# Attention and mixer on one core: fillers moved to a bank of their own, transposes and weight loads moved by a place

## The chip, the cores and the metric

The kernel runs on one core of a Trainium2 chip. The metric is the device time of one launch in microseconds (us). The engines are named as the profile names them: PE (TensorE, matrix multiplications; PEld is its loading of weights), DVE (VectorE), ACT (ScalarE), POOL (GpSimd) and SP (which here only starts transfers). POOL also starts transfers: those of the weights.

## What is computed

The reference, cut to what matters:

```python
q_n, k_n = rmsnorm(q, g_q), rmsnorm(k, g_k)          # (8, 12, 448, 64)
attn = softmax(q_n @ k_n^T / 8)                       # per batch and head
x = (attn @ v) as (8, 448, 768)
h = x^T @ U @ V                                       # rank 32, over the 448 tokens
u = x + h^T
out = u + relu(u @ w_ch1) @ w_ch2                     # 768 -> 3072 -> 768
```

Matrix multiplications run in bf16 and accumulate in fp32; inputs and output are fp32.

## The kernel before

**Stages.** Eight batches pass through attention, mixing (the rank-32 product) and the two-layer perceptron. The perceptron of batch b is PE's main work; the attention of batch b+1 is cut into small pieces that are woven into it. `weave` does that: it emits pieces of the perceptron (six matmuls each) until their volume reaches the share that is due by the weights of the attention's pieces, then one piece of the attention. The fraction of the perceptron over which a batch's attention is spread is `FA` (0.74 for even batches, 0.77 for odd), and `FM` (0.09) is that of the mixing that follows it. Each engine executes its own instructions in the order in which they were emitted; the program is scheduled by hand.

**The head.** Batch 0 has no perceptron to be woven into. Its order is a list written out by hand, `plan` in `head` (L659 to L867): normalise queries and keys (squares, reduce, rsqrt, scale), transpose them on PE (`turn`, L259, with the copies `keep`, L266), scores (L291), exponentials (`expo`, L301, on ACT), the product with the values (`weigh`, L307), its division by the sums (`normalise`, L327), and the mixing (`gather`, `spread`). `heat(n)` (L902) puts n fillers into PE's order: matmuls of zeros, 512 columns wide, whose result nobody reads. Each call takes a buffer of the pool `ps_mm`, which has three and which also serves transposes, products and the perceptron.

**A visit.** `attention(b)` (L575) emits six visits for a batch, one for each pair of heads p. A visit holds the scores for the four blocks of keys (two and two), their exponentials, the values of the pair before, and the preparation of the next pairs. `transposes(p)` turns the scaled queries and keys: on PE up to p = 13, by a transposing DMA from SP from p = 14 (`NPE`) on. Squares of heads 16 to 23 run on POOL (L233); later ones on ACT (L231).

**Two engines and one order.** `yield_port` (L568) is a copy of one element on POOL that reads what a `scale` on DVE (L253) writes, so that what stands behind it on POOL does not begin before that scale is done.

**Weights.** The first weights come in four loads, `load_w1(0)` to `load_w1(3)` (hidden columns up to 512, 1024, 2048 and 3072), the second in six, `load_w2`, all started by POOL. `load_w1(2)` holds what hidden blocks 8 to 15 of the perceptron need. The second weights 1 to 5 are started from the visits 6, 7 and 8 of batch 1's attention (`late`, L914).

**Mixing.** `mix_u` adds the low-rank term (DVE, L378); `mix_uT` turns each of the four blocks of rows by a transposing DMA from SP (L385). The perceptron of that batch begins with the result. Output blocks are stored by SP as well (`store`, L430).

**PSUM.** The pool `ps_o` has one bank; it holds `o`, the product with the values, 260 of the bank's 512 columns, before it is normalised.

Of the kernel before, what the change touches and what calls it, by code (L numbers as in the profile page):

```python
# [9 lines left out]
FP32 = mybir.dt.float32  # L10
# [7 lines left out]
def kernel(  # L18
# [13 lines left out]
    nc = tc.nc  # L32
    B, H, S, D = q.shape
# [5 lines left out]
    P = 128  # L39
# [26 lines left out]
    ps_mm = ctx.enter_context(tc.tile_pool(name="ps_mm", bufs=3, space=bass.MemoryType.PSUM))  # L66
    ps_s = ctx.enter_context(tc.tile_pool(name="ps_s", bufs=2, space=bass.MemoryType.PSUM))
    ps_o = ctx.enter_context(tc.tile_pool(name="ps_o", bufs=1, space=bass.MemoryType.PSUM))

    ident = consts.tile([P, P], BF16, name="ident")  # L70
    w1b = consts.tile([P, KD, dh], BF16, name="w1b")
# [17 lines left out]
    FA, FM, NPE, FA0, FL = (0.74, 0.77), 0.09, 14, 0.66, 0.2  # L89
# [20 lines left out]
    def E_of(p):  # L110
        return Es[p % 3 if p < 6 else p % 2]

    def va_of(t):
        return vas[t if t < 3 else (t + 1) % 2]
# [3 lines left out]
    cold = ring[:, 0, :]  # L118
# [73 lines left out]
    NT, NP = B * 3, B * 6  # L192
# [114 lines left out]
    def weigh(p, hh):  # L307

        b = p // 6
        par, g = b % 2, b // 2 % 2  # L310
        E, va = E_of(p), va_of(p // 2)
        hl = 2 * (p % 2) + hh
        if hh and p < 6:
            o = ps_mm.tile([P, 4, D + 1], FP32, tag="mm")
        elif hh and p % 6 == 5:
            o = ps_s.tile([P, 4, D + 1], FP32, tag="s", name="o")
        else:
            o = ps_o.tile([P, 4, D + 1], FP32, tag="o")
        for i, off in enumerate(OFFS[par]):
            n = (i + 1) % 4 if par == 0 and g else i  # L320
            for kc in range(NJ):
                c = PAD + kc * S + off
                nc.tensor.matmul(o[:, n, :], E[:, hh, c:c + P], va[:, hl, kc, :],  # L323
                                 start=(kc == 0), stop=(kc == NJ - 1))
        outs[p, hh] = o
# [18 lines left out]
    def values(p, hh):  # L344

        weigh(p, hh)
        normalise(p, hh)
# [227 lines left out]
    def attention(b, extra={}, later=None):  # L575

        items = []

        def add(weight, fn, *args):
            put = items if later is None or args[0] < ahead.get(fn, NP) else later  # L580
            put.append((weight, lambda: fn(*args)))

        def late_add(fn, *args):
            later.append((0, lambda: fn(*args)))

        def idle():
            pass

        def sums(p, n):
            f = {12: 0, 13: 1, 14: 3, 15: 2}.get(p)  # L590
            if f is not None:
                add(0, weight_sums, f, 3 * n)

        for p in range(b * 6, b * 6 + 6):
            t, odd = divmod(p, 2)
            more, more2 = t + 1 < NT, t + 2 < NT
            add(2 if p == 6 else 1, scores, p, (0, 1))
            add(0, expo, p, 0)
            add(.5, expo, p, 1)
            if p + 1 < NP and (p + 1 >= NPE or not odd):  # L600
                add(.5, transposes, p + 1)
            if 7 <= p <= 10:
                add(0, mix_u, 0, p - 7, (0,))
            sums(p, 0)
            lead = 1 if b == 1 else 2
            if not odd and p > 9 and t + lead < NT:
                add(0, load, t + lead, 1, (0,))
            if not odd and more:
                add(0, squares, t + 1, ALL, (1,))
            if odd and more2:  # L610
                add(0, squares, t + 2, ALL, (0,))
            if p % 6:
                add(2, values, p - 1, 0)
            elif b > 1:
                add(1, idle)
            sums(p, 1)
            if not odd and more:
                add(0, reduce, t + 1, ALL, (1,))
            if odd and more:
                add(0, scale, t + 1, 1)  # L620
                add(0, yield_port, t + 1, 1)
                add(0, cast_v, t + 1)
            if odd and 6 <= t + lead < NT:
                add(0, load, t + lead, 1, (1,))
            add(1, scores, p, (2, 3))
            add(0, expo, p, 2)
            add(.5, expo, p, 3)
            if p + 1 < NPE and odd:
                add(.5, transposes, p + 1)
            if 7 <= p <= 10:  # L630
                add(0, mix_u, 0, p - 7, (1,))
            if p + 1 < NP:
                add(0, gains, p + 1)
            if not odd and more:
                add(0, rsqrt, t + 1)
            sums(p, 2)
            if p % 6:
                add(1.5, values, p - 1, 1)
            elif b > 1:
                add(1, idle)  # L640
            sums(p, 3)
            if not odd and more:
                add(0, scale, t + 1, 0)
                add(0, yield_port, t + 1, 0)
            if odd and more2:
                add(0, reduce, t + 2, ALL, (0,))
            if odd and 6 <= t + lead < NT:
                add(0, load_v, t + lead)
            if p in extra:
                add(0, *extra[p])  # L650
            if p == 11:
                add(0, load, 7, 1, (0,))
                late_add(load, 7, 1, (1,))
                late_add(load_v, 7)
        add(2, values, b * 6 + 5, 0)
        add(2, values, b * 6 + 5, 1)
        return items

    def head():  # L659
# [13 lines left out]
        cast_u = lambda: nc.gpsimd.tensor_copy(Uc, Uf)  # L673
        pool = nc.gpsimd
        plan = [
            (heat, 16),
            (grow2,),
            (squares, 0, A, (0,), pool),
            (squares, 0, A, (1,)),
            (squares, 0, Bh, (0,), pool),  # L680
            (reduce, 0, A, (0,)),
            (reduce, 0, A, (1,)),
# [2 lines left out]
            (squares, 0, Bh, (1,)),  # L685
            (scale, 0, 0, (1,)),
            (reduce, 0, Bh, (1,)),
            (scale, 0, 0, (0,)),
            (rsqrt, 0, Bh),
            (scale, 0, 1, (1,)),  # L690
# [3 lines left out]
            (keep, 0, 0, 1),  # L694
            (yield_port, 0, 1),
            (squares, 1, ALL, (1,)),
            (keep, 0, 1),
            (scale, 0, 1, (0,)),
            (heat, 4),
            (scores, 0, (0,)),  # L700
            (turn, 1),
            (squares, 2, ALL, (0,)),
# [2 lines left out]
            (scores, 0, (1,)),  # L705
            (reduce, 1, ALL, (1,)),
            (load_w1, 0),
            (expo, 0, 1),
            (rsqrt, 1),
            (heat, 2),  # L710
            (scores, 0, (2,)),
            (scores, 0, (3,)),
            (keep, 1, 1),
# [2 lines left out]
            (squares, 2, ALL, (1,)),  # L716
            (scale, 1, 0, (0,)),
            (expo, 0, 2),
            (scale, 1, 1, (1,)),
            (heat, 5),  # L720
            (scores, 1, (0,)),
            (turn, 2),
            (scale, 1, 1, (0,)),
            (expo, 0, 3),
            (cast_u,),
            (expo, 1, 0),
            (scores, 1, (1,)),
            (scores, 1, (2,)),
            (load, 4),
            (heat, 2),  # L730
            (turn, 3),
# [5 lines left out]
            (expo, 1, 3),  # L737
            (scores, 2, (0,)),
            (yield_port, 1, 0),
            (scores, 2, (1,)),  # L740
            (cast_v, 0),
            (expo, 2, 0),
            (expo, 2, 1),
            (reduce, 2, ALL, (0,)),
            (reduce, 2, ALL, (1,)),
            (setup_u, 0),
            (scores, 2, (2,)),
            (scores, 2, (3,)),
# [141 lines left out]
    def weave(fill, total, items):  # L890
        weights = sum(w for w, _ in items)
        done = due = 0.0
        for w, piece in items:
            due += w * total / max(weights, 1)
            while done < due:
                n = next(fill, None)
                if n is None:
                    break
                done += n
            piece()  # L900

    def heat(n):  # L902
        if n:
            warm = ps_mm.tile([P, 512], FP32, tag="mm")
            for _ in range(n):
                nc.tensor.matmul(warm, cold[:, 0:P], cold[:, 0:512], start=True, stop=True)

    def volume(b):
        n = (384, 512)[b % 2]
        return (24 if b else 20) * n + (28 if b % 2 else 22 if b else 24) * HALF  # L910

    with tc.manual_schedule():
        head()
        late = {6: (load_w2s, 1, 3), 7: (load_w2s, 3, 5), 8: (load_w2s, 5, 6)}  # L914
        for b in range(B):
            fill, total = mlp(b), volume(b)
            if b + 1 < B:
                later = []
                rest = [(4, lambda: (load_w2(0, 0), transposes(6), reduce(4, ALL, (0,))))] + attention(1, late, later)
                weave(fill, total * (FA[b % 2] if b else FA0), attention(b + 1) if b else rest)  # L920
                weave(fill, total * FM, mixing(b + 1))
                if b == 0:
                    weave(fill, total * FL, [(5 if w == .5 else 1, piece) for w, piece in later])
            for _ in fill:
                pass
# [30 lines left out]
```

## Time and profile before

| | |
|---|---|
| time before, median of 5 runs | 579.99 us (577.8 to 581.91) |
| the profiled execution: its time | 581.91 us |
| its span (first to last record) | 580.1 us |
| mean granted PE clock | 0.987 |
| busy: PE, DVE, ACT, POOL | 561.8, 389.5, 281.6, 80.1 us |
| matmuls, instructions in all | 4585, 11284 |
| moved by DMA | 67.22 MB, mean 116 GB/s |

The profiled execution is the slowest of the five, 1.92 us over their median. A row of a timeline gives the start, the duration, the engine, the line of the kernel, the operation with its output and inputs, the count, and, in brackets, how long the engine stood idle before and what ended that. In a table by windows, each engine has its busy time in the window with the number of its instructions, and PEclk is the clock granted to PE as a share of full speed. "DMA" there is the mean busy share of 16 DMA engines; it can pass 1 where packets overlap.

### The profile page before, as it was taken

The numbers are of one execution on the slowest core, as the hardware profiler recorded it, in microseconds if no ns is written. First come the engines' busy times: TensorE is split into PE (matmuls) and PEld (weight loads), VectorE is DVE, ScalarE is ACT, GpSimd is POOL, SyncE is SP. The second block draws the span as 40 slices with busy tenths as digits, with TensorE's granted clock in tenths as the row PEclk, the third lists the DMA queues.
The fourth block names the chain that finished last, engine by engine and source line by source line (L and its number), as shares of the span: only waits on it lengthen the run. The fifth ranks groups of instructions, "written<-read, shape, count | busy, mean of one in ns | idle before, by whom it ended". The sixth has DMA issues, their size and how long they took to land.

```text
span 580.1 us, 11284 instructions
## 1 busy us (share of the span) xinstructions
PE 561.8 (97%) x4585; PEld 307.6 (53%) x4607; DVE 389.5 (67%) x755; ACT 281.6 (49%) x419; POOL 80.1 (14%) x124
## 2 busy tenths in 40 slices
PE   6798999999999999999999999999999999999997
PEld 2364555544565555544456555544456555654464
DVE  5885874889975687747777498747767487453342
ACT  4686554276631786166651677246661475302200
POOL 4672610100020000000020000000001000000010
PEclk9689999999999999999999999999999999999999
DMA  9999994445544455544525444455234541050021
GB/s 207 223 243 230 211 165 124 98 124 113 127 113 99 112 131 114 128 118 112 128 63 116 116 129 112 121 142 128 69 81 129 130 97 33 28 110 1 1 55 55
DMA packets 103648, 67.22 MB, mean 116 GB/s; under 512 B 54716, under 2 KB 102060, under 8 KB 103596
## 3 DMA queue, kind: packets, MB, share of 16 engines
q1 hardware_dynamic: 93988, 56.77, 41.4%
q0 software_dynamic: 9376, 9.44, 9.8%
q8 instruction: 36, 0.59, 0.4%
q10 hardware_dynamic: 232, 0.30, 0.1%
q14 instruction: 16, 0.13, 0.1%
HBM read 52.19 MB, written 11.01 MB: 109 GB/s over the span
## 4 chain that ended last, share of the span: by engine, by line
PE 83%; DVE 5%; DMA 5%; ACT 2%; issue 1%; SPq 0%; POOL 0%; DVEq 0%; ACTq 0%
PE ph L538 35%; PE pb L463 10%; PE o L323 8%; PE pe L463 7%; PE pa L463 7%; PE sc L297 7%; PE po L463 7%; DMA w1b<-in_moe_w_ch_dram 3%; DVE qkn L253 2%; PE pu L376 2%; ACT E L302 1%; DVE ring L378 1%; DMA qk<-in_q_dram 1%; DMA u<-ring 1%; DVE rstd L239 1%
## 5 line engine op out<-in xcount | busy, mean ns | idle before, releaser
L538 PE MATMUL ph<-u,w1b 128*128 128x384 bf16 (+1 forms) x1107 | 230.8, 353 | 4.5 <-DVE qkT L275 1.2
L302 ACT ACTIVATE E<-sc 112x896 bf16<-112x896 f32 x184 | 160.0, 915 | 63.6 <-PE sc L297 63.5
L538 PEld LDWEIGHTS <-w1b 128*128 128x128 bf16 x1128 | 102.9, 98 | 111.6 <-issue 23.2
L463 PEld LDWEIGHTS <-hT 128*128 128x128 bf16 x1080 | 101.1, 98 | 71.1 <-issue 9.0
L541 ACT ACTIVATE hT<-ph 128x384 bf16<-128x384 f32 (+1 forms) x95 | 51.6, 543 | 131.3 <-PE ph L538 129.2
L543 DVE TENSOR_SCALAR hT<-ph 128x512 bf16<-128x512 f32 (+1 forms) x93 | 57.8, 622 | 56.6 <-PE ph L538 56.4
L323 PEld LDWEIGHTS <-E 112*128 112x128 bf16 x1472 | 59.8, 99 | 14.7 <-DVE ring L340 1.1
L253 DVE TENSOR_TENSOR qkn<-qk,rstd 112x512 bf16<-112x512 f32 x84 | 58.4, 733 | 7.2 <-ACT rstd L245 3.8
L323 PE MATMUL o<-va,E 112*128 112x65 bf16 x1440 | 62.1, 196 | 0.0
L297 PE MATMUL sc<-qkT 64*128 64x448 bf16 x384 | 56.7, 365 | 3.6 <-ACT E L302 1.7
L570 POOL COPY scratch<-qkn 1x1 bf16<-1x1 bf16 x44 | 11.6, 264 | 314.1 <-DVE qkn L253 314.1
L463 PE MATMUL po<-w2b,hT 128*128 128x384 bf16 x288 | 52.8, 326 | 0.1
L239 DVE TENSOR_REDUCE rstd<-sq 112x16 f32<-112x1024 f32 x40 | 48.4, 1211 | 5.1 <-ACT sq L231 5.1
L463 PE MATMUL pa<-w2b,hT 128*128 128x384 bf16 x264 | 49.5, 326 | 0.0
L463 PE MATMUL pb<-Tw,hT 128*128 128x384 bf16 x264 | 48.0, 326 | 0.0
L231 ACT ACTIVATE sq<-qk 112x1024 f32<-112x1024 f32 x36 | 38.2, 1062 | 8.1 <-DVE rstd L239 5.2
L378 DVE TENSOR_TENSOR ring<-pu,ring 128x768 bf16<-128x768 f32 (+3 forms) x36 | 31.0, 864 | 14.4 <-PE pu L376 13.8
L340 DVE TENSOR_TENSOR ring<-o,rec 128x256 bf16<-128x256 f32 (+1 forms) x96 | 37.5, 391 | 2.4
L333 DVE RECIPROCAL rec<-o 128x4 f32<-128x4 f32 x96 | 17.1, 178 | 32.5 <-PE o L323 32.0
L498 POOL TENSOR_TENSOR o<-o,ring 128x384 f32<-128x384 f32 x11 | 12.6, 1145 | 161.4 <-DVE o L497 161.4
L297 PEld LDWEIGHTS <-qkT 64*128 64x128 bf16 x384 | 12.6, 94 | 35.6 <-issue 32.0
L478 ACT ACTIVATE pb<-pa 128x384 f32<-128x384 f32 x11 | 5.2, 475 | 49.6 <-PE pa L463 49.6
(104 smaller groups left out, 428.3 us busy)
## 6 DMA issues: line engine op xcount, KB each, us to landing
qk<-in_k_dram SPq DMA_DIRECT2D x21, 448.0 KB, 5.2
vt<-in_v_dram SPq DMA_DIRECT2D x20, 448.0 KB, 4.5
qk<-in_q_dram SPq DMA_DIRECT2D x19, 448.0 KB, 3.8
w2b<-in_moe_w_ch_dram POOLq DMA_DIRECT2D x6, 768.0 KB, 15.7
w1b<-in_moe_w_ch_dram POOLq DMA_DIRECT2D x2, 1536.0 KB, 18.7
out_dram<-o SPq DMA_DIRECT2D x15, 168.0 KB, 2.3
out_dram<-o SPq DMA_DIRECT2D x16, 144.0 KB, 2.2
out_dram<-o SPq DMA_DIRECT2D x15, 120.0 KB, 2.1
```

The costliest lines, as they stand in the source:

```text
L231: nc.scalar.activation(sqs[t, s][:, hs], qks[t, s][:, hs], AF.Square)
L239: nc.vector.tensor_reduce(rstds[t][:, s, hs].rearrange("p h j -> p (h j)"), sqs[t, s][:, hs].rearrange("p h (j d) -> p (h j) d", d=D), AX, ...
L253: nc.vector.tensor_tensor(qkn[:, s].rearrange("p j h d -> p h j d"), qks[t, s][:, hp].rearrange("p h (j d) -> p h j d", d=D), rstd[:, s, h ...
L297: nc.tensor.matmul(sc[:, hh, 0:S], kT[pp, kc * SP:kc * SP + P], qT[pp, :], start=True, stop=True)
L302: nc.scalar.activation(E_of(p)[:, :, PAD + kc * S:PAD + (kc + 1) * S], scs.pop((p, kc))[0:SP, :, 0:S], AF.Exp, scale=float(D) ** 0.5)
L323: nc.tensor.matmul(o[:, n, :], E[:, hh, c:c + P], va[:, hl, kc, :], start=(kc == 0), stop=(kc == NJ - 1))
L340: nc.vector.tensor_tensor(ring[:, r0:r0 + t1 - t0, d0:d0 + D], o[:, t0:t1, 0:D], rec[:, t0:t1].rearrange("p c -> p c ()").to_broadcast([P, ...
L378: nc.vector.tensor_add(xv, pu[rows, 0:n, 0:HALF], xv)
L463: nc.tensor.matmul(ps, lhs[:, c, :], rhs[:, c, :], start=first and c == 0, stop=last and c == NC - 1, skip_group_check=again)
L538: nc.tensor.matmul(ph, w1b[:, dc, hc * P:(hc + 1) * P], u[:, dc, :], start=(dc == 0), stop=(dc == KD - 1))
L541: nc.scalar.activation(hT[:, hc, 0:n], ph, AF.Relu)
L543: nc.vector.tensor_relu(hT[:, hc, 0:n], ph)
```

## The change

- **Fillers.** `o` of the pool `ps_o` becomes the first 260 columns of a fixed bank, and the fillers write columns 272 to 511 of that bank, 240 wide, instead of taking a buffer of `ps_mm`. Their counts and places in `plan` are new: 29 fillers of 512 columns become 117 of 240. In PE's order before the first product with the values there are now 49 before the first transpose, 11 before the first scores, then 5, 18, 13, 8, 9 and 4 between the scores and transposes that follow. No filler stands behind a product with the values.
- **Transposes by DMA.** From p = 14 on, `transposes(p + 1)` stands ahead of the first two scores of visit p, and its weight (0.5) with it; it stood behind them. So the scores stand half a weight later within the visit, which moves most of them one piece of six matmuls back.
- **Second weights.** Loads 1 to 5 stand behind the squares of a visit and ahead of the values, in visits 7, 8 and 9, where they ended visits 6, 7 and 8. On POOL this swaps each pair of loads with the square that followed it: load, load, square becomes square, load, load, at two places. The fifth load keeps its place among POOL's instructions.
- **The last attention.** The attention of batch 7 is spread over 0.72 of the perceptron of batch 6, not 0.74.

On PE the rest of the head keeps its order. In the last mixing, all four blocks of `mix_u` stand one piece of six matmuls earlier, and on SP the fourth transpose of `u` stands ahead of two output stores that it followed. DVE then adds the last block before the difference L490 and the sum L492, where it came after them.

```diff
+    bank = ps_o.tile([P, 512], FP32, name="bank")
+    even = bank[:, 0:4 * (D + 1)].rearrange("p (i d) -> p i d", i=4)
+    warm = bank[:, 272:512]
...
-            o = ps_o.tile([P, 4, D + 1], FP32, tag="o")
+            o = even
...
         for p in range(b * 6, b * 6 + 6):
...
+            if NPE <= p + 1 < NP:
+                add(.5, transposes, p + 1)
             add(2 if p == 6 else 1, scores, p, (0, 1))
             add(0, expo, p, 0)
             add(.5, expo, p, 1)
-            if p + 1 < NP and (p + 1 >= NPE or not odd):
+            if p + 1 < NPE and not odd:
                 add(.5, transposes, p + 1)
...
             if odd and more2:
                 add(0, squares, t + 2, ALL, (0,))
+            if p in extra:
+                add(0, *extra[p])
             if p % 6:
                 add(2, values, p - 1, 0)
...
-            if p in extra:
-                add(0, *extra[p])
...
         plan = [
-            (heat, 16),
+            (heat, 34),
...
+            (heat, 6),
...
+            (heat, 9),
...
             (squares, 1, ALL, (1,)),
+            (heat, 11),
...
-            (heat, 4),
...
             (load_w1, 0),
+            (heat, 5),
...
-            (heat, 2),
...
             (expo, 0, 2),
+            (heat, 18),
             (scale, 1, 1, (1,)),
-            (heat, 5),
             (scores, 1, (0,)),
             (turn, 2),
             (scale, 1, 1, (0,)),
             (expo, 0, 3),
+            (heat, 9),
+            (heat, 3),
             (cast_u,),
+            (heat, 1),
             (expo, 1, 0),
             (scores, 1, (1,)),
             (scores, 1, (2,)),
+            (heat, 1),
+            (heat, 5),
             (load, 4),
             (heat, 2),
             (turn, 3),
...
             (scores, 2, (0,)),
             (yield_port, 1, 0),
+            (heat, 9),
             (scores, 2, (1,)),
...
+            (heat, 4),
             (setup_u, 0),
...
     def heat(n):
         if n:
-            warm = ps_mm.tile([P, 512], FP32, tag="mm")
             for _ in range(n):
-                nc.tensor.matmul(warm, cold[:, 0:P], cold[:, 0:512], start=True, stop=True)
+                nc.tensor.matmul(warm, cold[:, 0:P], cold[:, 0:240], start=True, stop=True)
...
-        late = {6: (load_w2s, 1, 3), 7: (load_w2s, 3, 5), 8: (load_w2s, 5, 6)}
+        late = {7: (load_w2s, 1, 3), 8: (load_w2s, 3, 5), 9: (load_w2s, 5, 6)}
...
-                weave(fill, total * (FA[b % 2] if b else FA0), attention(b + 1) if b else rest)
+                weave(fill, total * (0.72 if b == B - 2 else FA[b % 2] if b else FA0), attention(b + 1) if b else rest)
```

## The prediction

> **What bounds the kernel now.** I read the windows of ten us first, then what PE waited for, then the chain of work. From 80 us on PE is busy 99% of the time at full clock, up to the last batch. So nothing before 500 us is won unless PE stops waiting, and its waits after 40 us are few. The view of waits, PE alone, from 40 us to the end (engine, line, waited for: us in total, times, longest):
>
> ```profile
> PE ph L538 <- DVE qkT L275: 1.2, 2, 1.0
> PE ph L538 <- DMA w1b<-in_moe_w_ch_dram: 0.9, 1, 0.9
> PE ph L538 <- DMA u<-ring: 0.9, 1, 0.9
> PE sc L297 <- ACT E L302: 0.7, 1, 0.7
> PE ph L538 <- DVE hT L543: 0.5, 1, 0.5
> ```
>
> That is 4.2 us in all. The head, which most of the edits touch, shows its trouble in windows of its own (start:end, length, then busy PE, PEld, DVE, ACT, POOL, PEclk, DMA share, GB/s):
>
> ```profile
> 15.37:18.78 3.41, 1.64 (x8) 0.59 (x7) 3.41 (x4) 2.91 (x5) 3.39 (x3) 1.00 1.13 180
> 18.78:32.43 13.65, 11.94 (x112) 6.97 (x113) 11.06 (x21) 8.20 (x12) 6.91 (x10) 0.50 1.13 240
> 32.43:52.50 20.07, 20.07 (x277) 13.21 (x274) 14.52 (x35) 14.74 (x27) 10.25 (x9) 1.00 1.14 239
> ```
>
> PE is idle from 17.11 to 19.77; at 18.78 its clock halves, and stays halved to 32.43: 13.65 us at half speed. It looks like the prize. But the chain shows what stands behind it:
>
> ```profile
> 36.02 17.39 DMA w1b<-in_moe_w_ch_dram
> 53.40 0.05 issue
> 53.45 1.16 PE ph L538 x6
> ```
>
> Hidden block 8 needs the third load of the first weights, which lands at 53.40, and PE, which got there at 52.55, waits for it.
>
> **Fillers: the landing does not move.** POOL's four loads follow each other on one queue: issued at 16.21, 29.76, 36.02 and 43.39 and landing 13.8, 13.6, 17.4 and 19.9 us later, at 30.0, 43.4, 53.4 and 63.3. Each starts when the one before is done, so the third would have to be issued after 43.4 to come later, and an earlier issue brings nothing. The first is issued behind a square that waited for its data (POOL idle 3.94 for the DMA of keys), the second behind casts that waited for theirs; no step waits for PE. DMA's share is above 1 from 10 to 80 us. So what the head gains up to 53.4 becomes a longer wait there: worth between nothing and the 0.90 us of the wait itself, should the load come sooner in other executions. The ends lie close; I take the middle, **0.45**.
>
> What the head gains is needed for a rival. A filler of 240 columns isn't in the trace: between 0.033 us (the product with 65 columns, 16 in 0.52) and 0.163 (384 columns, 12 in 1.95); by columns, nearer the second, 0.102, and double at half clock. The first 49: cold as now until about 8.5, then full, ending near 10.9 (between 6.3 and 13.8) where 16 ended at 9.4. The transpose then ends 1.4 us later, but its copy on ACT stands at 11.41 behind a square that ends at 11.51 because its data came at 10.45; without that cover it would cost 1.4. The next 11 put the first scores 0.4 late, behind an exponential that waits for ACT until 13.5. The 18 fill 15.5 to 17.3 and shorten the idle time of 2.65 us to 2.0. Thirteen then delay the scores (1,1) by 1.33 us less what the clock gives the transpose. If the clock holds, ACT's nine exponentials of 0.86 and two steps of rsqrt bound the stage, and DVE is held to 29.5 by POOL's casts as now: some 1 to 1.4 us gained at 33. If it falls all the same, fillers at 0.2 us make it 1 us later, of which the wait of 0.9 covers nearly all. The fillers end before the first product in the shared bank, so they add no wait; those they took from `ps_mm` go.
>
> **Loads behind the squares.** The timelines of POOL and DVE, from two calls:
>
> ```profile
> 59.69 1.83 POOL L189 DMA_DIRECT2D w2b<-in_moe_w_ch_dram  x2
> 61.53 1.91 POOL L233 TENSOR_TENSOR sq<-qk 112x1024 f32<-112x1024 f32 x1
> ```
>
> ```profile
> 61.51 3.09 DVE L253 TENSOR_TENSOR qkn<-qk,rstd 112x512 bf16<-112x512 f32 x2
> ```
>
> Two scales take 3.09 here and 1.29 at 58.10: they stand still while POOL squares. DVE then runs without a gap, and PE waits for its copies (L275), 0.96 at 64.36 and 0.25 at 68.6. With the square first it runs from 59.65 to 61.55, before the scales, and the two issues of 1.83 beside them; that issuing alone doesn't hold them shows at 44.28, where four scales beside an issue take 2.49, 0.62 each. The copies come 1.7 us sooner, and both waits go: **1.21** (between 0 and 1.21). Next late would be DVE's relu at 79.05 (0.45); I leave it. The loads start 2 us later, the second pair 2 to 3 more because the square ahead of it waits for a reduce: behind them wait a port copy and a cast. The queue is then still busy with the load that lands at 67.7, and the products that need the last three begin near 104, where DMA's share falls after 80: no cost. If the queue did run dry, the first products at 83.4 have some 6 us left.
>
> **Spread of 0.72.** The last mixing is one piece (0.98) earlier, DVE adds the fourth block ahead of L490 and L492 (0.96 and 0.55), and SP turns it ahead of two stores (0.99). Now it is this (SP's timeline):
>
> ```profile
> 508.16 4.18 SPq L385 DMA_TRANSPOSE u<-ring  x3
> 512.44 0.99 SPq L430 DMA_DIRECT2D out_dram<-o  x2
> 513.52 1.21 SPq L385 DMA_TRANSPOSE u<-ring  x1
> ```
>
> It lands at 517.70 and PE waits from 516.88. At least 2 us sooner, it ends the wait: **0.86**; the stores move 1.2 us back, and nobody waits for them.
>
> **Transposes ahead of the scores.** Each issue (1.22) passes two output stores at most on SP and then waits for its scale, as it does now; behind it stand loads for a later visit. DVE's two waits for such transposes, 3.7 us, are off the path. What counts is where the scores come to stand. Batches 2 and 4 have one piece between two pairs of scores, PE's timeline:
>
> ```profile
> 193.12 1.15 PE L538 MATMUL ph<-u,w1b 128*128 128x384 bf16 x6
> 194.38 0.80 PE L297 MATMUL sc<-qkT 64*128 64x448 bf16 x4
> ```
>
> The scores begin 0.19 late and take 0.25 longer than the usual 0.55, since ACT has not read the buffers: 0.44, and the same at 327.4. In the new order two pieces stand there, as in batch 6 at 461.69, where nothing is lost. But ACT has a square and a relu in between, so a rest may stay: between 0 and 0.88, I take **0.70**. Elsewhere the pieces stay two or more.
>
> **Sum.** 0.45 + 1.21 + 0.86 + 0.70 = 3.22 us. The profiled execution, 581.91, would be 578.7; it lies 1.92 above the median, and taken from the median, 579.99, the sum gives **576.8**.
>
> [...] The clock stayed at half for 13.65 us though PE's rows were busy 11.94 of them, and it fell after 1.67 us of idle time. [...]
>
> **Rivals.** (1) *The clock falls in the longer wait*, slower. If the head gains 1 to 1.4, PE stands idle 1.9 to 2.3 us ahead of 53.4, more than the 1.67 after which it fell; a wait shorter than that would not decide. A fall costs half of its length: 2.7 (the first fillers, dense, were cold for 5.4) to 6.8 (half of 13.65): 579.5 to **583.6**. Against it: 11.95 to 15.37 has 1.1 us of idle time and kept its clock, and dense hidden blocks stand on both sides. Chance 0.15, with 0.06 above 582.9.
> (2) *The landing isn't the bound* in most executions; the five spread over 4.1 us. Then the head's 1.4 counts, not 0.45: 579.99 - 2.77 - 1.4 = **575.8**, down to 574.5. Chance 0.17.
> (3) *The change doesn't do what it says*: the square still meets the scales, or the new weave makes waits as large as those it removes. Then 0.86 and 0.45 are left: **578.7**. The square ends only 0.04 ahead of the scales. Chance 0.22.
> The forecast (576.2 to 577.6) has 0.46.
>
> **Numbers.** A difference of 0.5%, 2.9 us, is about what a measurement of this kernel can tell from no change; that line, 577.1, cuts through the forecast. Faster: 0.33 of the forecast and rival 2, 0.50. Slower: 0.06. The rest, 0.44, within. The range goes from 574.8 to 579.6: it leaves out rival 1 but for its low end, and the lowest of rival 2.
>
> **What would show it.** Right: PEclk 1.00 from 18 to 32 us and a longer wait for `w1b`, ending near 53.4; the scales near 61.5 at 1.3; no wait on the copies of `qkT` near 64; no wait on `u` near 515; batches 2 and 4 without late scores. Wrong: the third load landing earlier or later by over 1 us, a half clock after 50, or new waits of PE between 120 and 500 us.

## The result, and the profile after

The changed kernel takes **577.2 us** (median of 37 runs, 574.88 to 579.89); the kernel before, run beside it on the same chip, 579.84 (577.4 to 582.82). The ratio is 0.9953, with a 95% interval of 0.9943 to 0.9963: 2.6 us, or 0.47%, faster. A second measurement in another set of runs (e10 below) gave 577.01 and 0.995 [0.9931, 0.997]. The profiled execution took 576.35 us, its span is 574.6 us, its mean granted clock 1.000.

What PE waited for from 40 us to the end, as in the first list of the prediction:

```profile
PE ph L541 <- DMA u<-ring: 1.1, 1, 1.1
PE sc L300 <- ACT E L305: 0.7, 1, 0.7
PE ph L541 <- DVE hT L546: 0.4, 1, 0.4
```

The copies of `qkT` (1.2) and the first weights (0.9) are gone from it. The wait for `u` is still there, and longer; it is another one, though: it stood ahead of batch 7 and now stands ahead of batch 5, whose order in the mixing is not changed. The windows of the head (columns as in the prediction) have no half clock any more:

```profile
10.00:20.00 10.00, 7.96 (x81) 5.87 (x79) 8.60 (x12) 6.92 (x10) 6.24 (x6) 1.00 1.13 240
20.00:30.00 10.00, 9.99 (x138) 6.91 (x136) 7.81 (x18) 8.22 (x12) 4.37 (x7) 1.00 1.15 251
```

The squares and loads on POOL, and the scales on DVE, from two timelines:

```profile
56.12 1.89 POOL L236 TENSOR_TENSOR sq<-qk 112x1024 f32<-112x1024 f32 x1
57.95 1.83 POOL L192 DMA_DIRECT2D w2b<-in_moe_w_ch_dram  x2
```

```profile
58.03 1.28 DVE L256 TENSOR_TENSOR qkn<-qk,rstd 112x512 bf16<-112x512 f32 x2
```

The square ends at 58.01, the scales begin at 58.03 and take 1.28 instead of 3.09, beside the two issues. This is what the prediction described, to the order of 0.02 us. PE's timeline where batch 2 lost 0.44 us with one piece between two pairs of scores:

```profile
185.05 0.55 PE L300 MATMUL sc<-qkT 64*128 64x448 bf16 x4
185.54 2.12 PE L541 MATMUL ph<-u,w1b 128*128 128x384 bf16 x12
187.59 0.55 PE L300 MATMUL sc<-qkT 64*128 64x448 bf16 x4
```

Two pieces (2.12) stand there now, and the scores take 0.55.

How much earlier the same point of PE's work is reached than in the profile before: hidden block 0 of batch 0 by 2.5 us, block 8 by 3.5, the first product with the second weights by 5.0, the start of batch 1 by 5.0, of batch 3 by 5.6, of batch 5 by 4.9 (the new wait), of batch 7 by 5.6, the end by 5.5. That is twice what the medians show, because the two profiled executions are a late and an early one: the third load of the first weights landed at 53.4 in the one and at 49.8 (33.49 + 16.3) in the other. Whether the fillers brought any of that is open: three profiles below with the old fillers have it at 50.4 to 52.6, four with the new ones at 49.1 to 50.2 (this one among them) and a fifth at 53.1.

### The profile page after: what moved, and what is told of

Read it like the earlier page. It is cut to its first block, busy times and chain, and to the rows that moved or that the text cites. A ratio compares the mean times of both kernels' runs of the same rounds, so it can differ in the third digit from the quotient of the medians.

```text
span 574.6 us, 11445 instructions
## 1 busy us (share of the span) xinstructions
PE 561.7 (98%) x4674; PEld 314.0 (55%) x4695; DVE 385.7 (67%) x755; ACT 282.1 (49%) x419; POOL 78.9 (14%) x124
## 4 chain that ended last, share of the span: by engine, by line
PE 92%; DVE 3%; DMA 1%; ACT 1%; issue 0%; DVEq 0%; ACTq 0%
PE ph L541 38%; PE pb L466 10%; PE po L466 8%; PE sc L300 8%; PE bank L326 7%; PE pe L466 7%; PE pa L466 7%; PE pu L379 2%; PE o L326 1%; DVE qkn L256 1%; DMA u<-ring 1%; PE first L893 1%; PE pt L267 1%; PE bank L919 1%; DVE ring L381 1%; PE pm L365 1%
## 5 line engine op out<-in xcount | busy, mean ns | idle before, releaser
L256 DVE TENSOR_TENSOR qkn<-qk,rstd 112x512 bf16<-112x512 f32 x84 | 54.3, 685 | 3.9 <-ACT rstd L248 2.3
L300 PE MATMUL sc<-qkT 64*128 64x448 bf16 x384 | 54.7, 354 | 1.3 <-ACT E L305 0.7
L326 PE MATMUL bank<-va,E 112*128 112x65 bf16 x1280 | 54.1, 194 | 0.0
L343 DVE TENSOR_TENSOR ring<-bank,rec 128x192 bf16<-128x192 f32 (+1 forms) x83 | 32.3, 389 | 1.9
L336 DVE RECIPROCAL rec<-bank 128x4 f32<-128x4 f32 x83 | 14.8, 179 | 27.5 <-PE bank L326 27.2
```

Source lines behind the costliest of these rows:

```text
L256: nc.vector.tensor_tensor(qkn[:, s].rearrange("p j h d -> p h j d"), qks[t, s][:, hp].rearrange("p h (j d) -> p h j d", d=D), rstd[:, s, h ...
L300: nc.tensor.matmul(sc[:, hh, 0:S], kT[pp, kc * SP:kc * SP + P], qT[pp, :], start=True, stop=True)
L343: nc.vector.tensor_tensor(ring[:, r0:r0 + t1 - t0, d0:d0 + D], o[:, t0:t1, 0:D], rec[:, t0:t1].rearrange("p c -> p c ()").to_broadcast([P, ...
```

## The experiments

The theory after the result (Q): in the head the landing of the third load, not PE, sets when hidden block 8 can begin; so the fillers are worth nothing, and the gain is that of the moved loads and transposes. The main rival (H): the head's own work counts in most executions, and the clock that the fillers hold is worth 1 us or more. Each set of runs has its own runs of the kernel before, on the same chip: 580.6 us in the first (e1 to e4), 579.97 in the second (e5, e7 to e9), 579.79 in the third (e10 to e13). There is no e6. Ratios are to those, with 95% intervals; they are not quotients of the two medians, and gains of e1 to e4 in us are taken from the ratios.

### e1 to e4: one part of the change alone

Each is the kernel before with one part of the diff above. e1 has the bank and the new fillers:

```diff
-            (heat, 16),
+            (heat, 34),
...
+                nc.tensor.matmul(warm, cold[:, 0:P], cold[:, 0:240], start=True, stop=True)
```

> The kernel before with the fillers' part alone (the shared bank, the new counts and places). Theory Q, as in the prediction: the third load of the first weights lands by its queue, whatever the head does, so the gain is 0 to 1 us, ratio 0.998 to 1.000, and PE waits for that load longer than 0.9 us. Rival H: the landing is not what holds the head; the time gained ahead of it stays, 2 to 3.5 us, ratio 0.994 to 0.9965, and PE reaches hidden block 8 near 50 us without a wait. Both: the clock is full from 18 to 32 us in most executions.

Measured: 580.2 us (577.86 to 582.09), ratio 1.0002 [0.998, 1.0023]. Its runs show clocks of 0.994 to 1.000, those of the kernel before 0.987 to 0.997, so with the new fillers the clock holds longer, and no gain shows; the interval leaves room for 1.2 us, less than H asks for. In its profile, that of its fastest run, the load lands at 49.1 and PE comes to hidden block 8 at 49.7 without a wait, which is H's picture and not Q's.

e2 has the loads behind the squares:

```diff
-        late = {6: (load_w2s, 1, 3), 7: (load_w2s, 3, 5), 8: (load_w2s, 5, 6)}
+        late = {7: (load_w2s, 1, 3), 8: (load_w2s, 3, 5), 9: (load_w2s, 5, 6)}
```

> The kernel before with the loads of the second weights behind the squares, alone. As in the prediction: two scales near 61.5 us take 1.3 us instead of 3.1, PE's two waits for the copies of qkT (0.96 and 0.25) go: 1.2 us, ratio 0.998. Rival: the square still meets the scales, or the load's wait for the first weights covers it: ratio 1.000.

Measured: 579.01 us (577.75 to 581.41), 0.9983 [0.9964, 1.0002], some 1.0 us, with no change just inside the interval. No wait on `qkT` is left in its profile. The same profile shows the clock falling without a long wait (columns as in the prediction):

```profile
21.48:24.89 3.41, 2.00 (x21) 0.95 (x21) 2.90 (x6) 3.38 (x7) 2.25 (x4) 1.00 1.18 237
24.89:28.30 3.41, 3.41 (x47) 2.59 (x45) 3.28 (x7) 2.38 (x4) 2.90 (x4) 0.50 1.16 260
```

In the 3.41 us ahead of the fall at 24.89 PE was busy for 2.00, and no idle stretch was longer than 0.44; an idle stretch of 2.56 that ended at 19.18 had not halved it.

e3 has the transposes ahead of the scores:

```diff
+            if NPE <= p + 1 < NP:
+                add(.5, transposes, p + 1)
             add(2 if p == 6 else 1, scores, p, (0, 1))
```

> The kernel before with the DMA transposes ahead of the scores, alone. As in the prediction: 0.7 us in batches 2 and 4, ratio 0.9988. Rival: other places of the new weave lose as much: ratio 1.000 or above, with new waits of PE between 120 and 500 us.

Measured: 578.49 us (576.17 to 581.93), 0.9981 [0.9958, 1.0004], some 1.1 us, with no change just inside the interval. From the first block of batch 2 to that of batch 3 PE takes 60.19 us, where the kernel before takes 60.80; from batch 4 to batch 5 it is 60.19 against 60.77. So each of the two batches gains 0.6, 1.2 in all.

e4 has the spread of 0.72:

```diff
-                weave(fill, total * (FA[b % 2] if b else FA0), attention(b + 1) if b else rest)
+                weave(fill, total * (0.72 if b == B - 2 else FA[b % 2] if b else FA0), attention(b + 1) if b else rest)
```

> The kernel before with the last attention spread over 0.72, alone. As in the prediction, if the wait for the last transpose of u stands in every execution: 0.86 us, ratio 0.9985. Rival L: that transpose lands 2.8 us after its issue in most executions and 4.2 to 4.4 in some, and only those wait: 0.1 to 0.3 us, ratio 0.9995 to 1.000. Both: no wait for u at the start of the last batch.

Measured: 580.04 us (577.08 to 585.16), 1.0002 [0.9975, 1.0029]. The wait for `u` is gone in its profile, but the denser attention makes in batch 6 what the old order had in batches 2 and 4, one piece between two pairs of scores:

```profile
461.83 1.15 PE L538 MATMUL ph<-u,w1b 128*128 128x384 bf16 x6
463.10 0.80 PE L297 MATMUL sc<-qkT 64*128 64x448 bf16 x4
```

Batch 6 to batch 7 takes 60.82 us here, 60.10 in e1, which has the old spread and had no wait there. So by the profiles the spread alone costs 0.7 and saves a wait of 0.86. Its profile shows something else as well, in the head: the wait for the third load at its worst, and the clock that falls in it, as rival 1 had it (PE's timeline, then the windows).

```profile
52.65 2.10 PE L538 MATMUL ph<-u,w1b 128*128 128x384 bf16 x6 [2.83 <-DMA w1b<-in_moe_w_ch_dram]
```

```profile
50.00:60.00 10.00, 7.07 (x40) 3.71 (x41) 4.92 (x9) 5.47 (x10) 2.23 (x3) 0.83 1.15 224
```

Six matmuls that take 1.15 at full clock take 2.10 behind the 2.83 us of idle time.

### e8 and e9: the first weights earlier

e8 is the kernel before, and e9 the changed kernel, with the first three loads of the first weights issued earlier:

```diff
             (turn, 1),
+            (load_w1, 0),
             (squares, 2, ALL, (0,)),
...
-            (load_w1, 0),
...
             (cast_u,),
+            (load_w1, 1),
...
             (setup_v,),
+            (load_w1, 2),
...
-            (load_w1, 1),
...
-            (load_w1, 2),
```

> The kernel before with the first three loads of the first weights issued earlier on POOL: the first ahead of the square before it, the second behind the cast of the mixing matrix, the third behind a piece of set-up. Nothing else is changed. Theory Q (the queue: each starts when the one before is done): the third lands about 1.9 us sooner (as much as the first is issued sooner), near 51.5, the wait for it goes, and the time falls by 0.5 to 0.9 us, to 579.1 to 579.5. Theory D (all loads share what DMA moves, so an earlier issue takes from keys and values what it gives to weights): the landing stays within 0.7 us of 53.4 or the head is as much later, and the time is within 0.4 us of 579.99.

> The changed kernel with the same earlier issues of the three loads. Theory Q: in the executions in which the third load was late it no longer is, so the fillers' gain in the head now counts: 1.0 to 1.5 us below the changed kernel, 575.7 to 576.2, and the difference to the kernel before with early loads is larger than that of the change itself (2.7 us) by 0.5 us or more. Theory D: within 0.5 us of 577.2, and no such surplus.

Measured: e8 578.79 us (577.58 to 579.87), 0.9973 [0.9957, 0.9989]; e9 576.42 us (575.37 to 576.71), 0.9933 [0.9912, 0.9955]. The first load is issued at 11.48 in e8 and 11.07 in e9, over 4 us sooner, since it no longer stands behind a square that waits for keys; the third lands at 47.5 and 45.7, and the wait for it is gone. So D fails: an earlier issue does bring the load sooner, in e8 by 4 us more than Q expected (51.5). Which of the three issues did it is not separated, since all three moved. But Q expected a surplus for e9, and there is none: by the medians e8 gains 1.2 us on the kernel before and e9 0.6 to 0.8 on the changed one, by the ratios 1.6 (0.6 to 2.5) and 1.0 to 1.2, where the intervals of e9 and of the changed kernel overlap.

Do the loads wait for each other's landing, as the prediction has it? The second load does not: it lands 12.5 to 14.4 us after its own issue in all fourteen profiles, whether the first landed 0.3 us after that issue (kernel before) or 7.4 (e11). Nor does the third strictly: in the kernel before, the queue of these loads had moved 2.03 MB by 43.37, when the second landed, and the first two make 1.57. But by the landings its data stands behind theirs: issued at 36.02, when 1.15 MB had been moved, it landed 10.0 us after the second, and 9.9 to 11.3 after it in nine of the ten profiles with this order of issues.

### e7 and e11: no fillers behind the first 49

e7 is the changed kernel without the later 68 fillers (the first 49 stay; the 40 in its expectation is a slip), e11 the same with the early loads of e9:

```diff
-            (heat, 11),
...
-            (heat, 5),
...
-            (heat, 18),
...
-            (heat, 9),
-            (heat, 3),
```

(and the six behind those).

> The changed kernel with the first 40 fillers and none of the later ones. Theory Q (up to the landing of the third load nothing that the head gains counts): the clock falls at 17 to 19 us and stays halved for some 10 us, mean clock .987 to .992, the head is 1 to 2 us later at 33 us, and the time is within 0.6 us of the changed kernel's, 577.2. Theory H (the head's own work counts in most executions): 1.0 to 2.0 us above it, 578.2 to 579.2.

> The changed kernel with the three loads issued earlier and without the fillers behind the first 49. Beside the changed kernel, the one without the later fillers and the one with early loads it makes a square of four. Theory Q (the late third load hides what the fillers gain): with early loads the fillers count, so this is 1.0 us or more above the changed kernel with early loads (576.4 in the call before), 577.4 or more, though without early loads they were worth nothing. Theory N (the fillers are worth nothing even where the load is in time, because something between 33 and 80 us takes their gain back): 576.0 to 577.0. The clock is .984 to .988 in both.

Measured: e7 576.54 us (575.74 to 578.03), 0.9941 [0.992, 0.9962], at clocks of 0.984 to 0.988; e11 **575.73** us (575.06 to 576.8), 0.9929 [0.9909, 0.995], at 0.984 to 0.987. e11 has the lowest median of all kernels here, though its interval overlaps that of the changed kernel. So with late loads and with early ones the kernel without these fillers is level with the kernel that has them, or some 0.5 us ahead. H fails, and so does Q's reason: the fillers don't count where the load is in time either. Theory N's number holds, but not its reason: nothing takes the gain back after 33 us, because at 33 us there is none. PE's timelines show why: e9 with the fillers, e11 without.

```profile
19.17 0.57 PE L267 MATMUL pt<-ident,qkn 112*128 112x112 bf16 x8 [1.27 <-DVE qkn L256]
19.57 1.50 PE L919 MATMUL bank<-ring 128*128 128x240 bf16 x13
21.00 0.55 PE L300 MATMUL sc<-qkT 64*128 64x448 bf16 x4
...
39.41 1.15 PE L893 MATMUL first<-u,w1b 128*128 128x384 bf16 x6
```

```profile
18.53 0.93 PE L267 MATMUL pt<-ident,qkn 112*128 112x112 bf16 x8 [1.06 <-DVE qkn L256]
19.39 0.93 PE L300 MATMUL sc<-qkT 64*128 64x448 bf16 x4
...
39.19 1.15 PE L882 MATMUL first<-u,w1b 128*128 128x384 bf16 x6
```

At half clock the transposes take 0.93 instead of 0.57, but their scores follow at once; at full clock thirteen fillers stand between, and the scores come 1.6 us later. ACT, which had nothing to do until these scores, is late with them. DVE pays a second time, by its scale (its timelines, e9 and then e11):

```profile
26.39 2.13 DVE L256 TENSOR_TENSOR qkn<-hT,rstd 112x512 bf16<-112x512 f32 x2
```

```profile
24.80 1.29 DVE L256 TENSOR_TENSOR qkn<-hT,rstd 112x512 bf16<-112x512 f32 x2 [0.36 <-issue]
```

In e11 it ends as POOL's cast begins (26.09 and 26.03); in e9 it meets POOL's port copy and cast and takes 0.84 longer. Hidden block 0 (`first`) begins at 39.41 and 39.19: level, with the clock at 1.00 from 10 to 40 us in e9 and at 0.79 and 0.53 in the first two windows of ten in e11.

What puts e11 ahead of e9 lies later. Batch 1 begins at 109.39 in e9 and 109.16 in e11, batch 5 at 378.19 and 376.95: e9 waits 0.84 us for `u` there, and e11 does not, for a reason that e5 led to.

### e5: more fillers

```diff
             (scores, 1, (0,)),
+            (heat, 17),
             (turn, 2),
```

> The changed kernel with 17 more fillers in the one long idle stretch of PE that its head still has, 17.4 to 19.3 us (1.7 us of fillers). Some runs of the changed kernel show a mean clock of 1.000 and a time near 576.4, the others .997 and 577 to 580. Theory A (the clock falls for one window in that idle stretch): nearly all runs now show 1.000, and the median falls by about 0.8 us, to 576.4. Theory B (it falls elsewhere, in the wait for the third load of the first weights): the shares stay as they are, and the median within 0.5 us of the changed kernel's, 577.2.

Measured: 575.87 us (575.14 to 578.3), 0.9932 [0.9909, 0.9955]; five of six runs show 0.999 or 1.000. By the numbers theory A. Its reason is neither shown nor refuted: the two profiles of the changed kernel show PEclk 1.00 across the same idle stretch (1.93 us in the first), but both are of executions with a mean clock of 1.000, and no profile of it shows one at 0.997. What e5's profile has lost, beside the changed kernel's, is the wait for `u` (its list from 40 us on):

```profile
PE sc L300 <- ACT E L305: 0.7, 1, 0.7
PE ph L541 <- DVE hT L546: 0.5, 1, 0.5
PE ph L541 <- DVE qkT L278: 0.2, 1, 0.2
```

That led to the transfers of that stretch. In the DMA view, cut to the 4.5 us from the issue of the last `u` transpose ahead of batch 5 in the changed kernel, the first two rows are busy tenths and GB/s in 40 slices:

```profile
DMA  9799853100299999997219999000000000079930
GB/s 218 232 273 328 273 178 109 41 14 0 41 196 223 221 218 196 362 214 139 37 59 218 205 96 41 0 0 2 7 9 9 9 7 14 14 273 396 356 82 0
...
q8 instruction: 1, 0.02, 1.7%
...
u<-ring SPq DMA_TRANSPOSE x1, 4.4
```

The transpose lands after 4.4 us. For ten slices, 1.1 us, DMA moves 0 to 14 GB/s, and a queue that the view calls instruction has one packet there. The same view of e5, from the issue of the same transpose:

```profile
q1 hardware_dynamic: 1683, 1.03, 75.6%
issues: line engine op xcount, KB each, median us to landing
...
u<-ring SPq DMA_TRANSPOSE x1, 2.8
```

No packet of the instruction queue, and it lands after 2.8. In all fourteen profiles, the last transposes ahead of batches 5 and 7 make 28 places. In eleven of them a packet of queue q8 begins 1.1 to 2.4 us after the issue; these are all the places where the landing is late (3.9 to 4.5 us where the view gives it), and in nine of them PE waits for `u`, 0.6 to 1.2 us. In the other two, batch 7 of e7 and e11, the transpose lands after 4.5 and 4.4 as well, but the spread of 0.72 has issued it so early that PE does not wait. In the other seventeen there is no wait; in one of them (batch 5 of e12) a packet stands just ahead of the issue and the landing takes 3.2, elsewhere 2.7 to 2.8 where it is given. The place is the same from profile to profile: with the 29 old fillers or the first 49 alone, the packet comes at the start of batch 7 (before, e2, e3, e8, e7, e11; in e4, with the earlier turn, just behind the landing), with the 117 new ones ahead of batch 5 (changed kernel twice, e1, e9, e13), with 134 (e5) at neither. So it does not look like chance: in these profiles the packet's place goes with the number of fillers that PE has had before. The last transposes ahead of batches 2 and 4 meet a packet in ten more places and land after 3.4 to 3.8 us; PE waits at none of these.

### e12, e13 and e10

e12 is e9 with e5's fillers and with 0.72 for all even batches; e13 is the changed kernel with the old spread of the last attention; e10 is the changed kernel itself.

```diff
-                weave(fill, total * (0.72 if b == B - 2 else FA[b % 2] if b else FA0), attention(b + 1) if b else rest)
+                weave(fill, total * ((0.72 if b % 2 == 0 else FA[1]) if b else FA0), attention(b + 1) if b else rest)
```

> The changed kernel with the early loads, the 17 more fillers in the idle stretch of 17 to 19 us, and the spread of 0.72 for all even batches instead of the sixth alone. If the waits for u at the starts of batches 5 and 7 are worth what single profiles show (0.5 to 1.1 us each, in about every other execution): no wait on u, 574.8 to 575.5. If the earlier turn only moves the wait elsewhere: 575.8 to 576.5, like the kernels with one of the edits. Either way it should be the fastest so far or level with it.

> The changed kernel with the old spread of the last attention. If the spread is worth its 0.86 in most executions: 0.5 to 0.9 us above the changed kernel of this call, with a wait for u at the start of batch 7 of 0.5 us or more. If the wait came by chance, as other profiles suggest: within 0.4 us of it.

> The changed kernel itself, unaltered, as the measure for the three others of this call: 577.2 us as before, within 0.6.

Measured: e12 577.99 us (576.0 to 580.38), 0.9956 [0.9937, 0.9976]; e13 577.99 us (576.73 to 580.5), 0.9964 [0.9945, 0.9983]; e10 577.01 us (575.68 to 579.25), 0.995 [0.9931, 0.997].

e12 misses both of its theories: it has no wait for `u`, and is 1.6 us slower than e9. Batch 2 takes 60.82 us to the start of batch 3 instead of 60.20, and batch 4 the same, for the reason seen in e4 (one piece ahead of scores, which then wait 0.25 for ACT). That is 1.2 us, of which the wait saved gives back 0.84. The remaining 1.2 us between the medians I can't place.

e13 is 1.0 us above e10, but the intervals overlap, and its profile has no wait ahead of batch 7 and 60.20 us from batch 6 to 7, where e10 takes 60.48: by the profiles the spread costs 0.3 in this kernel. Its runs show the lower mean clock, 0.997, in nine of twelve, e10's in one of seven. Its profile has a mean clock of 1.000 and doesn't show where that clock is lost, so what the spread is worth in the whole change stays open.

e10's profile tells most of the third load. Its list of waits from 40 us on:

```profile
PE ph L541 <- DMA w1b<-in_moe_w_ch_dram: 2.4, 1, 2.4
PE ph L541 <- DMA u<-ring: 0.9, 1, 0.9
PE sc L300 <- ACT E L305: 0.7, 1, 0.7
PE ph L541 <- DVE hT L546: 0.4, 1, 0.4
```

The same code that did not wait for this load in one execution waits 2.4 us for it in another; it landed at 53.1, and the clock stayed at 1.00.

## Why the prediction was right, and where it was not

The time is 0.4 us off, and the sign and the reasons for most of the gain hold; that it is so near is in part luck. One term was too small, for one no worth shows, and one rests on something that the prediction did not see. Two of its own signs of being wrong came in the profile: the third load landed at 49.75 and not near 53.4, and a new wait of 1.1 us stands at 378 us. The third, a half clock after 50 us, came in e4.

- **Loads behind the squares, 1.21.** Right in mechanism and size. The scales take 1.28, both waits on the copies of `qkT` are gone in e2 and in the changed kernel, and e2 alone measures 1.0 us, with an interval from none to 2.1.
- **Transposes ahead of the scores, 0.70 of at most 0.88.** Right in mechanism, too small: e3 shows 0.61 and 0.58 us in batches 2 and 4, 1.2 in all. The late scores of 0.44 were counted; some 0.16 in each batch I have not traced to a row.
- **Fillers, 0.45.** No gain shows (e1, 1.0002, within 1.2 us), and e7 and e11 do as well or better without most of them. The step that failed is the gain of 1 to 1.4 us in the head, taken from the clock. "ACT's nine exponentials of 0.86 and two steps of rsqrt bound the stage" was written there, and with it the fillers that stand ahead of the scores cost as much as the clock gives. The half clock was also sized by one execution, the slowest of five: it lasts 13.65 us there, 10.24 in e8 and only 3.41 in the heads of e2 and e4, all with the old fillers. Hidden block 0 begins at 38.6 to 41.7 us in the five profiles with the old fillers and at 38.9 to 39.8 in the seven with the new. The queue was read too strictly as well: the loads don't wait for each other's landing, and the landing that "does not move" lay at 49.1 to 53.4 with the same order. Rival 2, the landing that isn't the bound, is half right: of the ten profiles with this order, five wait for the load (0.9 to 2.8 us) and five do not. But the gain that rival 2 built on it, the head's 1.4, is not there.
- **Spread, 0.86.** The wait ahead of batch 7 is gone, as predicted, and was there in each profile with the old fillers and the old spread. But what stood beside it was a packet of the queue q8, and in all fourteen profiles no wait for `u` ahead of batches 5 and 7 came without one, so the position of the transpose alone does not make it. With the 117 fillers of the same change that packet stood no longer at batch 7 (e1 and e13 have no wait there with the old spread) but ahead of batch 5, where PE waits 0.6 to 1.2. The denser attention costs 0.3 to 0.7 of its own. Without the later fillers the spread does what it was costed for: in e7 and e11 the packet is back at batch 7, and the earlier turn hides it. As a saving of the whole change the term is not shown.
- **Rival 1** happens: in e4 the clock fell in the wait for the third load, for 3.41 us, which by estimate (half of that length) can cost 1.7 at most and not the 2.7 that the rival gave as its least. In e10 it did not, after 2.45 us of idle time, and at 17 us it fell after 1.88 us in e8 (PEclk 0.51 from 20 to 30) and not after 1.93 us in the changed kernel. So neither the trace's 1.67 us as a threshold, which the prediction used, nor a bare length of idle time tells when it falls. What the traces do show is how long the clock stayed halved: 3.41 us (e2 and e4), 10.24 (e8) and 13.65 (kernel before), 1, 3 and 4 times the same length. It may be that the clock changes only in steps of that length, and that where in such a step the idle time falls counts; that is a guess from these lengths and was not tried. How much 3.41 us at half clock may be worth can be estimated from the runs of the changed kernel: with the profiled one, 21 of 38 have a mean clock of 0.999 or 1.000 and a median of 576.6 us, the other 17 have 0.996 to 0.998 and 578.3. By estimate, 3.41 us at half clock in a span of 575 makes 0.997 and costs 1.7 us, which is the difference; where it falls in those runs no profile shows.
- **Rival 3**, the square that still meets the scales, did not happen: 58.01 against 58.03, a margin that was 0.04 in the prediction and held in e2 as well.

The sum came out near because terms erred both ways: transposes 0.5 too small, fillers 0.45 too large, the spread uncertain.

## What to carry to other kernels

A half clock in a trace is not yet a loss: look at who is waited for in that stretch, and count what keeps the clock up as work in PE's queue, because in e9 thirteen fillers ahead of a product that ACT waits for brought the scores 1.6 us later than in e11, where the transposes took 0.93 us at half clock instead of 0.57. When two executions of one kernel differ by more than the change is worth, take the landing of each load on the path, and the length of a half clock, from several profiles before you put a saving on them. And an operation moved or added in one stage can move a collision in a far one, as the packet beside `u` went from batch 7 to batch 5 here (waits of 0.86 and 1.11 us): after the edit, read the whole list of waits again, not the stage alone.

## What the runs showed of the hardware that was not expected

**A queue that the view calls instruction, and transposes that land late.** The page of the changed kernel lists 37 packets on the queue that has a packet beside each late landing of `u` ahead of batches 5 and 7:

```profile
q8 instruction: 37, 0.61, 0.4%
```

Each is 16,384 bytes in the trace. What they hold no trace says. The changed kernel's trace has 4,674 matmuls and 4,695 weight loads, 253 rows of PE for each packet; that of the kernel before has 4,585 and 4,607 with 36 packets, 255 for each, while DVE, ACT and POOL have the same numbers of instructions in both (755, 419 and 124). That the packets are PE's instructions is an inference from this and from the place, which moves with the fillers. 0.4% of DMA's time looks like nothing, but where a packet began between the issue of a transpose of `u` and its landing, that took 3.4 to 4.5 us; elsewhere it took 2.7 to 2.8, and 3.2 in e12 with a packet just ahead of the issue. Of the eleven places ahead of batches 5 and 7 where a packet met the transpose, the delay was hidden in two, and in nine PE waited 0.6 to 1.2 us; the ten ahead of batches 2 and 4 were all hidden. That a few instructions shift a kernel out of the collision was seen in e5 (17 more fillers, landing after 2.8 us, no wait for `u`), whose fillers were meant for something else; it was not tried by itself.

**The same queue, other times.** The third load of the first weights, 1.5 MB, landed between 49.1 and 53.4 us in ten executions with the same order of issues. With the three loads issued earlier (e8, e9, e11, e12: the first by 4 us or more, the third at 28.5 to 30.5 instead of 33.0 to 36.0) it landed between 45.7 and 47.5, ahead of its use in all four.
